# Turns by PE's transpose mode, a 64-row attention tile by pairs of heads, a decay term read from SBUF, and ranks averaged in the planner

## The chip, the core and the metric

One core of a Trainium2 chip. The metric is the device time of one execution in microseconds (us). Engines: PE (TensorE; PEld is its weight load), DVE (VectorE), ACT (ScalarE), POOL (GpSimd), SP (SyncE, whose queue issues the DMAs).

## What is computed

Attention with a decay, then two MLPs, for 4 x 576 tokens. Cut to what matters:

```
scores = q @ k.T / 8 + cum[:, None] - cum[None, :]    # 4 batches, 8 heads, 576 rows, 64 wide; cum = cumsum(log(clip(f)))
attn   = softmax(causal(scores)) @ v                  # float32 inputs
h = x @ w_in;  x = (h * tanh(softplus(h))) @ w_out    # 512 -> 2048 -> 512, weights float64
h = x @ w2_in; s = h * softmax(h)                     # 512 -> 1024 -> 512
out = (layernorm(s) * g_ln) @ w2_out
```

cum of the query row is the same for a whole row of the softmax, so only the key's part, -cum, is added.

## The kernel before, in words

Tokens stand in tiles of 128 rows. Each batch has five tiles of queries (NCH); in batch 0 the last one has 64 rows. `seq` lists attention steps (batch, tile, heads): four heads at a time in the first tile, two in the second, one in the others. Each step runs `step_s` (scores, L511), `step_r` (row maximum on DVE, exponentials on ACT, L535), `step_h` (the probabilities cut into two fp16 halves by ACT and POOL, then transposed by a DMA, L570) and `step_pv` (products with v, L607); `fin` (L640) divides by the row sums, cuts the result and transposes it by DMA into `xT`, the input of the first MLP.

Batch 0 is special. Its q and k are fp32 and are turned by `turn` (L394): PE multiplies a block by the fp32 identity (L399), ACT copies the result from PSUM (L403, L405). In its first two tiles the probabilities are turned in the same way. Scores are a group of products in `scores` (L479): q by k in fp32 (L500), then the decay (L501) as an fp16 product of 67 rows, of which 64 are zero and three are ones (`qb`) that meet the three fp16 parts of -cum in rows 64 to 66 of `ktr`, one row set a head; on the diagonal the mask is added by an identity product (L505). The decay is made on chip by a scan (L268), cut into three fp16 parts, written to DRAM (`dd`, L274) and read back into `ktr` by a DMA for each key chunk (L414).

In the last tile of a batch the 64-column end of the keys has its own scores for all eight heads first (into `sps[2]`), then each head has 512 columns.

PE's other work: gram products of the weights (L148), the low halves of early weights (`h_lo`, L192 and L193), the first MLP (`up`, L887; `down`, L931), the second MLP (L1686, and L1763, where the output has seven products). DVE converts the float64 weights (L125 to L129).

The program is written in one order and then reordered: `Order` (L1108) models every operation's cost (`weigh`, `duration`), makes orders by a list schedule forward (`plan`) with ranks that a backward pass gives (`back`), twelve rounds at each of two slowdowns, replays every order found with random delays, and pins the order with the least time on each engine (`pin`, L1568). How much attention is put between the MLP's steps is set by `att_slots` from `cost` (L984). Engines run their own queues in the pinned order and wait on semaphores.

Of the kernel before, what the change touches and what calls it, by code (L numbers as in the profile page):

```python
# [211 lines left out]
def emit(tc, q, k, v, f, w_in, w_out, w2_in, w2_out, g_ln, out):  # L212
# [14 lines left out]
        fill=MASKED, base=0, channel_multiplier=1,  # L227
    )
    ones = const.tile([P, P], F32, name="ones")
    nc.gpsimd.memset(ones, 1.0)  # L230
# [35 lines left out]
    nc.vector.memset(ft, 1.0)  # L266
    dt_ = rp0.tile([B * H, S], F32, name="dt_")
    nc.vector.tensor_tensor_scan(dt_, ft, lf, 0.0, op0=ALU.mult, op1=ALU.subtract)  # L268
# [17 lines left out]
    for i in range(2):  # L286
        nc.gpsimd.memset(qb[i][64:96], 1.0)
    for t in q32:
        nc.gpsimd.memset(t[64:, :, 0], 0.0)
        nc.gpsimd.memset(t[:64, :, 1], 0.0)  # L290
# [103 lines left out]
    def turn(dst, src, r0, r1_, nm, scale=1.0):  # L394

        t = psh.tile([P, 2, TB], F32, tag="h", name=f"h_{nm}").rearrange("p g (y s) -> p (g y) s", s=P)
        n = src.shape[-1] // P
        for y in range(n):
            nc.tensor.matmul(  # L399
                t[:, y, r0:r1_], src[r0:r1_, y * P:(y + 1) * P], ident32[r0:r1_, r0:r1_], start=True, stop=True)  # L400
        if type(dst) is list:
            for y, d in enumerate(dst):
                nc.scalar.activation(d[:, :, r0:r1_], t[64 * y:64 * y + 64, :, r0:r1_], AF.Copy, scale=scale)  # L403
            return
        nc.scalar.copy(dst[:, :n, r0:r1_], t[:, :n, r0:r1_])  # L405

    def split_k(b, c):
        r0, r1_, t0 = rows_of(b, c)
        n = r1_ - r0
        if b == 0:  # L410
            x = (b * NCH + c) % NKT
            turn(kt32[:, x, :4], raw["k", b, c], r0, r1_, f"k{c}")
            kt[b, c] = ktr[:, x]
            nc.sync.dma_start(  # L414
                ktr[64:67, x, H:, r0:r1_],
                dd[b * H:(b + 1) * H, :, t0:t0 + n].rearrange("h j s -> j h s"),
            )
            return
        t = kn[cnt["kn"] % KNB]
        cnt["kn"] += 1  # L420
        t3 = t[:, :H * P].rearrange("p (h d) -> p h d", h=H)
        rk = hd(raw["k", b, c][r0:r1_])
        s = sc["k", b][r0:r1_]
        split(nc, t3[r0:r1_, :, 64:], t3[r0:r1_, :, :64], rk, s, qmode(b, c, 0))
        kc = ktr[:, (b * NCH + c) % NKT]
        kt[b, c] = kc
        nc.sync.dma_start_transpose(out=kc[:, :H, r0:r1_], in_=t[r0:r1_, :H * P])
        nc.vector.tensor_copy(kc[:64, H:, r0:r1_], kc[64:, :H, r0:r1_])  # L428
        nc.sync.dma_start(
            kc[64:67, H:, r0:r1_],  # L430
            dd[b * H:(b + 1) * H, :, t0:t0 + n].rearrange("h j s -> j h s"),
        )
# [13 lines left out]
    def split_q(b, c):  # L446
        r0, r1_, t0 = rows_of(b, c)
        if b == 0:
            qa = q32[c % 2]
            turn([qa[:64, :, 0], qa[64:, :, 1]], raw["q", b, c], r0, r1_, f"q{c}", 0.125)  # L450
            qt[b, c] = qa, qb[0]
            return
        t = attd.tile([P, H, P], F16, tag="qn", name=f"qn_{b}_{c}", bufs=1)
        rq = hd(raw["q", b, c][r0:r1_])
        s = sc["q", b][r0:r1_]
        split(nc, t[r0:r1_, :, :64], t[r0:r1_, :, 64:], rq, s, qmode(b, c, 2))
        qa = qat[:, cnt["qb"] % 2].rearrange("p (h s) -> p h s", s=P)
        nc.sync.dma_start_transpose(out=qa[:, :, r0:r1_], in_=t[r0:r1_].rearrange("p h d -> p (h d)"))
        qb_ = qb[cnt["qb"] % 2]
        cnt["qb"] += 1  # L460
        nc.vector.tensor_copy(qb_[:64, :, r0:r1_], qa[:64, :, r0:r1_])
        qt[b, c] = (qa, qb_)
# [16 lines left out]
    def scores(o, b, i, h, cs):  # L479

        r0, r1_, _ = rows_of(b, i)
        qa, qb_ = qt[b, i]
        for c0, c1 in runs(b, cs):
            a0, a1, _ = rows_of(b, c0)
            w = 128 * (c0 - cs[0])
            s = (b * NCH + c0) % NKT
            n = c1 - c0
            d = o[:, w + a0 - o0(b, cs):w + 128 * (n - 1) + a1 - o0(b, cs)]
            k = ktr[:, s:s + n]
            k2 = k[:67, :, H + h]  # L490
            if b:
                q1, k1 = qa[:, h, r0:r1_], k[:, :, h]
            else:
                q1, k1 = qa[:, h // 2, h % 2, r0:r1_], kt32[:, s:s + n, h // 2]
            if n > 1:
                d = d.rearrange("p (c s) -> p c s", s=P)
            else:
                k1, k2 = k1[:, 0, a0:a1], k2[:, 0, a0:a1]
            diag = c1 == i + 1
            nc.tensor.matmul(d, q1, k1, start=True, stop=False)  # L500
            nc.tensor.matmul(d, qb_[:67, h, r0:r1_], k2, start=False, stop=not diag)  # L501
            if diag:
                a0, a1, _ = rows_of(b, i)
                w = 128 * (i - cs[0]) - o0(b, cs)
                nc.tensor.matmul(o[:, w + a0:w + a1], ident[:, r0:r1_], maskd[:, a0:a1], start=False, stop=True)  # L505

# [4 lines left out]
    def step_s(b, i, hs):  # L511
# [5 lines left out]
        if i < NCH - 1:  # L517
# [3 lines left out]
            for g, h in enumerate(hs):  # L521
                cs = range(i + 1)
                o = sp[:m, wd * g + o0(b, cs):wd * (g + 1)]
                scores(o, b, i, h, cs)
        else:
            if hs[0] == 0:
                assert banks() == 3
                for h in range(H):
                    scores(sps[2][:m, 64 * h:64 * (h + 1)], b, i, h, [0 if off else i])
            sp = sps[cnt["s"] % 2]  # L530
# [4 lines left out]
    def step_r(b, i, hs):  # L535
# [13 lines left out]
        if i < NCH - 1:  # L549
# [6 lines left out]
            return  # L556
        h = hs[0]
        ex = sps[2][:m].rearrange("p (h s) -> p h s", h=H)
        if h == 0:
            ne = attd.tile([P, H], F32, tag="ne", name=f"ne_{b}", bufs=1)  # L560
            nc.vector.tensor_reduce(ne[:m], ex, axis=AX.X, op=ALU.max, negate=True)
            pend["ne", b] = ne
# [7 lines left out]
    def step_h(b, i, hs):  # L570
        m, pt = pend.pop(("p", b, i, hs))
        n = len(hs) * (i + 1)
        if b == 0 and i < 2:
            pT = attd.tile([P, 4 * NCH, P], F16, tag="pT", name=f"pT_{b}_{i}_{hs[0]}", bufs=PTB)
# [4 lines left out]
        h0, o = hs[0], 0  # L579
        if n == i + 1 and h0 % 2:  # L580
            h0 -= 1
            o = n
            ph = pend.pop(("ph", b, i))
        else:
            ph = attd.tile([P, 4 * NCH, P], F16, tag="ph", name=f"ph_{b}_{i}_{h0}", bufs=PHB)
# [12 lines left out]
        nc.gpsimd.tensor_tensor(p4[:, :, 1], pv3, p4[:, :, 0], op=ALU.subtract)  # L598
        if n == i + 1 and o == 0:
            pend["ph", b, i] = ph  # L600
            return
# [5 lines left out]
    def step_pv(b, i, hs):  # L607
# [20 lines left out]
        for g, h in enumerate(hs):  # L628
            o = acc[:m, h * D:(h + 1) * D]
            for c in range(i + 1):  # L630
                a0, a1 = (0, P) if i else rows_of(b, c)[:2]
                vc = vt[b, c]
                vh = vc[a0:a1, 0, h * D:(h + 1) * D]
                vl = vc[a0:a1, 1, h * D:(h + 1) * D]
                k = 2 * (g * (i + 1) + c)
                nc.tensor.matmul(o, pT[a0:a1, k, :m], vh, start=(c == 0), stop=False)  # L636
                nc.tensor.matmul(o, pT[a0:a1, k, :m], vl, start=False, stop=False)  # L637
                nc.tensor.matmul(o, pT[a0:a1, k + 1, :m], vh, start=False, stop=(c == i))  # L638

    def fin(b, i):  # L640
# [4 lines left out]
        rr = attd.tile([P, H], F32, tag="rr", name=f"rr_{b}_{i}", bufs=2)  # L645
        st = 1 if i == NCH - 1 else 2
        nc.vector.tensor_reduce(
            rr[:m], rs[:m, 0:3:st].rearrange("p j h -> p h j"), axis=AX.X, op=ALU.add)
        nc.vector.reciprocal(rr[:m], rr[:m])
        x32 = attd.tile([P, DM], F32, tag="x32", name=f"x32_{b}_{i}", bufs=1)  # L650
# [85 lines left out]

    seq = []
    for b in range(B):
        for i, g in enumerate(GRP):
            seq += [(b, i, tuple(range(h, h + g))) for h in range(0, H, g)]  # L740
    pos = {"k": 0, "pv": 0}

# [234 lines left out]
    for j in range(NBLK):  # L977
        last = (j + 1) * TB - 1
        b, t = divmod(last, S)
        i = (t + OFF[b]) // P  # L980
        need.append(b * sum(H // g for g in GRP) + sum(H // g for g in GRP[:i + 1]))
    assert need[0] == n0

    def cost(n):  # L984
        b, i, hs = seq[n]
        return (128 * (i + 1) + 60) * len(hs)

# [95 lines left out]
LANDED = 600.0  # L1083
ROUNDS = 12
SEEDS = 8
# [22 lines left out]
class Order:  # L1108
# [141 lines left out]
    def weigh(self):  # L1250

        for o in self.ops:
            if o.eng == "PE":
                o.rows = [next(b for t, b, w in acc if not w).ap[0][1] > 64 for i, acc in o.ins]
                o.d = SWITCH * sum(a != b for a, b in zip(o.rows, o.rows[1:]))
                for i, acc in o.ins:
                    c = elems(next(b for t, b, w in acc if w)) / 2.4
                    if size_of(next(t for t, b, w in acc if not w).dtype) == 4:
                        c = max(4.0 * c, 224.0)
                    o.cols += c  # L1260
# [307 lines left out]
    def pin(self):  # L1568
        found = []
        for f in SLOW:  # L1570
            self.slower(f)
            rank = [o.k for o in self.ops]
            for _ in range(ROUNDS):
                found.append(self.plan(rank))
                rank = self.back()
        self.slower(1.0)
# [261 lines left out]
```

## Time and profile before

| | us |
|---|---|
| median of 3 runs | 769.73 |
| lowest and highest | 769.17, 769.89 |
| profiled execution | 770.08 |
| its span, first to last instruction | 766.9 |
| PE busy in it | 736.0 |

Busy times are unions of instruction spans; a matmul's end is modelled, so matmuls in a row overlap in their spans, and what one of them costs is read from start to start. An fp32 product stands as two records. Granted clock 1.00 is 2.4 GHz, 0.50 is 1.2 GHz.

### The profile page before, as it was taken

How to read it: one execution, taken by the hardware profiler on the slowest of the kernel's cores; microseconds unless marked ns; L12 is line 12 of the kernel's file. 1: busy time of each engine (PE TensorE's matmuls, PEld its weight loads, DVE VectorE, ACT ScalarE, POOL GpSimd, SP SyncE). 2: the span in 40 equal slices, each digit the busy share in tenths (PEclk: the TensorE clock that was granted, in tenths of full speed). 3: DMA queues.
4: the chain of work that ended last, by engine and by line, in shares of the span. 5: the costliest groups of instructions: out<-in, count | busy, mean ns of one | idle time of the engine just before them, and what ended most of it. 6: DMA issues, size and time to landing. Idle time of an engine off the chain costs nothing.

```text
span 766.9 us, 17022 instructions
## 1 busy us (share of the span) xinstructions
PE 736.0 (96%) x6346; PEld 509.6 (66%) x6346; DVE 582.0 (76%) x1201; ACT 605.7 (79%) x1315; POOL 424.3 (55%) x368
## 2 busy tenths in 40 slices
PE   4999999999998999999999999999999999999898
PEld 3776765566675677766778777675754565566577
DVE  6988987888798887688778637798945776766564
ACT  3686999988998989998998968997766656767550
POOL 6013356577766786775787933314213565877721
PEclk9999999999998999999999999999999999999999
DMA  9979777899769999989988446530022678778765
GB/s 272 288 224 250 221 130 129 149 167 173 181 148 187 168 174 204 177 152 174 175 163 161 89 84 174 185 127 12 20 51 56 117 143 149 155 146 165 136 146 137
DMA packets 317118, 118.06 MB, mean 154 GB/s; under 512 B 302380, under 2 KB 303148, under 8 KB 317036
## 3 DMA queue, kind: packets, MB, share of 16 engines
q1 hardware_dynamic: 317036, 116.99, 73.0%
q8 instruction: 49, 0.80, 0.4%
q14 instruction: 33, 0.27, 0.1%
HBM read 46.59 MB, written 9.55 MB: 73 GB/s over the span
## 4 chain that ended last, share of the span: by engine, by line
PE 58%; ACT 10%; DMA 10%; DVE 9%; POOL 7%; issue 6%; SPq 0%; ACTq 0%; POOLq 0%; DVEq 0%
PE x L931 15%; PE h L887 15%; PE o L1763 7%; PE h L1686 5%; PE sp L500 4%; PE sp L501 2%; DMA win<-za 2%; DMA x2d<-x2h 2%; POOL s L1724 2%; POOL gt L914 2%; PE h_lo L192 2%; POOL ph L598 2%; DMA wi_r<-in_moe_w_in_dram 1%; DMA pT<-ph 1%; PE pv L636 1%
## 5 line engine op out<-in xcount | busy, mean ns | idle before, releaser
L931 PE MATMUL x<-wout,gt 128*128 128x512 f16 x864 | 214.7, 382 | 5.1 <-POOL gt L914 2.9
L887 PE MATMUL h<-xT,win 128*128 128x256 f16 x1728 | 210.2, 273 | 1.3 <-ACT th L900 1.3
L887 PEld LDWEIGHTS <-win 128*128 128x128 f16 x1728 | 166.5, 98 | 39.2 <-issue 2.9
L598 POOL TENSOR_TENSOR ph<-p,ph 128x512 f16<-128x512 f32 (+4 forms) x114 | 149.2, 1314 | 60.8 <-ACT ph L597 46.1
L914 POOL TENSOR_TENSOR gt<-th,gt 128x512 f16<-128x512 f32 x72 | 96.6, 1343 | 109.6 <-ACT gt L913 109.5
L931 PEld LDWEIGHTS <-gt 128*128 128x128 f16 x864 | 79.7, 98 | 78.4 <-issue 6.2
L1686 PE MATMUL h<-w,x2T 128*128 128x512 f16 x432 | 95.7, 379 | 0.1
L908 DVE SCALAR_TENSOR_TENSOR th<-ta,th 128x512 f32<-128x512 f32 x72 | 55.7, 774 | 25.9 <-ACT ta L907 21.6
L1686 PEld LDWEIGHTS <-x2T 128*128 128x128 f16 x432 | 42.1, 98 | 49.0 <-issue 0.7
L553 ACT ACTIVATE p<-sp,nm 64x64 f32<-64x64 f32 (+7 forms) x128 | 62.2, 492 | 7.9 <-DVE nm L551 6.0
L551 DVE TENSOR_REDUCE nm<-sp 128x1 f32<-128x320 f32 (+7 forms) x88 | 49.1, 564 | 24.0 <-PE sp L505 15.5
L899 ACT ACTIVATE ta<-h,cols 128x512 f32<-128x512 f32 (+3 forms) x96 | 54.3, 580 | 15.8 <-PE h L887 15.8
L659 POOL TENSOR_TENSOR xh<-x,xh 128x512 f16<-128x512 f32 (+1 forms) x20 | 27.9, 1394 | 65.1 <-DVE xh L658 64.7
L501 PE MATMUL sp<-ktr,qb 67*128 67x64 f16 (+6 forms) x304 | 59.5, 241 | 1.7 <-DVE ktr L428 1.7
L500 PE MATMUL sp<-ktr,qat 128*128 128x64 f16 (+7 forms) x288 | 54.3, 260 | 2.0 <-ACT p L568 2.0
L913 ACT CAST gt<-th 128x512 f16<-128x512 f32 x72 | 44.7, 621 | 11.3 <-DVE th L908 6.7
L904 DVE TENSOR_SCALAR ta<-ta 128x512 f32<-128x512 f32 x72 | 47.1, 655 | 8.7 <-ACT ta L899 8.1
L906 ACT ACTIVATE ta<-ta,cols 128x512 f32<-128x512 f32 x72 | 52.0, 723 | 0.5
L905 ACT ACTIVATE ta<-ta 128x512 f32<-128x512 f32 x72 | 45.5, 633 | 8.2 <-DVE ta L904 8.2
L636 PE MATMUL pv<-vt,pT 128*128 128x64 f16 (+2 forms) x456 | 50.2, 196 | 0.3 <-DMA pT<-ph 0.2
L638 PE MATMUL pv<-vt,pT 128*128 128x64 f16 (+2 forms) x456 | 50.0, 195 | 0.0
L637 PE MATMUL pv<-vt,pT 128*128 128x64 f16 (+2 forms) x456 | 50.0, 195 | 0.0
(272 smaller groups left out, 1641.6 us busy)
## 6 DMA issues: line engine op xcount, KB each, us to landing
wi_r<-in_moe_w_in_dram SPq DMA_DIRECT2D x8, 1024.0 KB
wo_r<-in_moe_w_out_dram SPq DMA_DIRECT2D x8, 1024.0 KB
x2d<-x2h SPq DMA_DIRECT2D x18, 256.0 KB
out_dram<-ro SPq DMA_DIRECT2D x18, 256.0 KB
w2i_r<-in_moe_w_in_dram SPq DMA_DIRECT2D x4, 1024.0 KB
w2o_r<-in_moe_w_out_dram SPq DMA_DIRECT2D x4, 1024.0 KB
rawv<-in_v_dram SPq DMA_DIRECT2D x13, 256.0 KB
rawk<-in_k_dram SPq DMA_DIRECT2D x13, 256.0 KB
```

What stands on the lines that cost most here:

```text
L500: nc.tensor.matmul(d, q1, k1, start=True, stop=False)
L501: nc.tensor.matmul(d, qb_[:67, h, r0:r1_], k2, start=False, stop=not diag)
L553: nc.scalar.activation(pv[:m, g * (i + 1) * P + off:g * (i + 1) * P + end], s3[:, g, off:end], AF.Exp, bias=nm[:m, g:g + 1], accum_out=rs[ ...
L598: nc.gpsimd.tensor_tensor(p4[:, :, 1], pv3, p4[:, :, 0], op=ALU.subtract)
L636: nc.tensor.matmul(o, pT[a0:a1, k, :m], vh, start=(c == 0), stop=False)
L887: nc.tensor.matmul(ph, win[:, (fi // 4) * NC1 + c, col:col + P], x[:, lx * NC1 + c, :], start=(m == 0), stop=(m == 3 * NC1 - 1))
L899: nc.scalar.activation(ta[:, :, a:e], ph[:, :, a:e], AF.Exp, scale=usc(b, fi // 4))
L908: nc.vector.scalar_tensor_tensor(th, ta, 2.5, th, op0=ALU.subtract, op1=ALU.mult)
L914: nc.gpsimd.tensor_tensor(gt[:, 1], th, gt[:, 0], op=ALU.subtract)
L931: nc.tensor.matmul(o, gt[:, lg, n % 2, t * P:(t + 1) * P], wout[:, fi, lw * 512:(lw + 1) * 512], start=(first and m == 0), stop=(last and ...
L1686: nc.tensor.matmul(h[:, half * 512:(half + 1) * 512], x[:, lx * NC1 + c, :], self.w2[:, half * NC1 + c, lw * 512:(lw + 1) * 512], start=(n ...
L1763: nc.tensor.matmul(o, z[nm][:, (2 * at + lz) * q + c, :], self.wo[:, form, lw, c], start=(n == 0), stop=(n == 3 * q - 1))
```

## The change

- `turn` uses PE's transpose mode in place of a product with the identity.
- Batch 0's last tile: two heads are stacked, one in rows 0 to 63 and one in rows 64 to 127. The q turn puts the even head's 64 rows at columns 64 to 127 of its block, so that 128 neighbouring columns hold both heads. The decay then has six rows, three a head, and `pick`, a block of ones in `qb[0]`, gives each half its three; the DMA of the decay writes six rows for four pairs. `mask2` is the 64-wide mask twice. Maxima, exponentials, halves and transposes run once a pair; `fin` brings the pair's reciprocals back to 64 rows. `qb[0]` is set to ones again before batch 1 uses it.
- The first two tiles take their decay from the scan's fp32 tile in SBUF, padded with zeros to 128 rows, by a product with one column of the identity broadcast to 128; their key chunks are no longer taken together.
- The planner: a transpose counts 112 ns, the ranks are the mean of the last four backward passes, and there are twenty rounds.

The diff, without its context lines:

```diff
@@ -226,6 +226,9 @@
+    mask2 = const.tile([P, D], BF16, name="mask2")
+    for y in range(0, P, D):
+        nc.vector.tensor_copy(mask2[y:y + D], maskd[y:y + D, y:y + D])
@@ -264,7 +267,10 @@
-    dt_ = rp0.tile([B * H, S], F32, name="dt_")
+    dtp = rp0.tile([P, S], F32, name="dt_")
+    for y in range(B * H, P, B * H):
+        nc.gpsimd.memset(dtp[y:y + B * H, :2 * P], 0.0)
+    dt_ = dtp[:B * H]
@@ -285,6 +291,11 @@
+    pick = qb[0][:70, :2].rearrange("p h s -> p (h s)")
+    for i, (m, o) in enumerate(((-1, 2), (1, -3))):
+        x = qb[0][64:96, i]
+        nc.gpsimd.affine_select(
+            out=x, in_=x, pattern=[[0, P]], compare_op=ALU.is_ge, fill=0.0, base=o, channel_multiplier=m)
@@ -396,11 +407,11 @@
-            nc.tensor.matmul(
-                t[:, y, r0:r1_], src[r0:r1_, y * P:(y + 1) * P], ident32[r0:r1_, r0:r1_], start=True, stop=True)
+            nc.tensor.transpose(t[:, y, r0:r1_], src[r0:r1_, y * P:(y + 1) * P], ident32[r0:r1_, r0:r1_])
-                nc.scalar.activation(d[:, :, r0:r1_], t[64 * y:64 * y + 64, :, r0:r1_], AF.Copy, scale=scale)
+                o = 0 if y or r1_ == P else P - r1_
+                nc.scalar.activation(d[:, :, r0 + o:r1_ + o], t[64 * y:64 * y + 64, :, r0:r1_], AF.Copy, scale=scale)
@@ -412,8 +423,8 @@
-                ktr[64:67, x, H:, r0:r1_],
-                dd[b * H:(b + 1) * H, :, t0:t0 + n].rearrange("h j s -> j h s"),
+                ktr[64:70, x, H::2, r0:r1_],
+                dd[b * H:(b + 1) * H, :, t0:t0 + n].rearrange("(x y) j s -> (y j) x s", y=2),
@@ -448,7 +459,7 @@
-            qt[b, c] = qa, qb[0]
+            qt[b, c] = qa, pick
@@ -457,6 +468,8 @@
+        if (b, c) == (1, 1):
+            nc.gpsimd.memset(qb_[64:96, :2], 1.0)
@@ -480,29 +493,37 @@
-        for c0, c1 in runs(b, cs):
+        for c0, c1 in runs(b, cs) if b or i > 1 else [(c, c + 1) for c in cs]:
-            k2 = k[:67, :, H + h]
+            one, low = ident[:, r0:r1_], maskd
-                q1, k1 = qa[:, h, r0:r1_], k[:, :, h]
+                q1, k1, q2, k2 = qa[:, h, r0:r1_], k[:, :, h], qb_[:67, h, r0:r1_], k[:67, :, H + h]
-                q1, k1 = qa[:, h // 2, h % 2, r0:r1_], kt32[:, s:s + n, h // 2]
+                x, y = divmod(h, 2)
+                q1, q2 = qa[:, x, y, r0:r1_], qb_[:, y * P + r0:y * P + r1_]
+                if i == NCH - 1:
+                    q1, q2 = qa[:, x].rearrange("p y s -> p (y s)")[:, D:D + P], qb_[:, D:D + P]
+                    one, low = ident, mask2
+                k1, k2 = kt32[:, s:s + n, x], k[:70, :, H + 2 * x]
+                if i < 2:
+                    q2 = ident32[:, h:h + 1].to_broadcast([P, P])
+                    k2 = dtp[:, c0 * P:c1 * P].rearrange("p (c s) -> p c s", s=P)
-            nc.tensor.matmul(d, qb_[:67, h, r0:r1_], k2, start=False, stop=not diag)
+            nc.tensor.matmul(d, q2, k2, start=False, stop=not diag)
-                nc.tensor.matmul(o[:, w + a0:w + a1], ident[:, r0:r1_], maskd[:, a0:a1], start=False, stop=True)
+                nc.tensor.matmul(o[:, w + a0:w + a1], one, low[:, a0:a1], start=False, stop=True)
@@ -523,10 +544,13 @@
+            if b == 0:
+                m = P
-                for h in range(H):
-                    scores(sps[2][:m, 64 * h:64 * (h + 1)], b, i, h, [0 if off else i])
+                for h in range(0, H, len(hs)):
+                    x = h // len(hs)
+                    scores(sps[2][:m, 64 * x:64 * (x + 1)], b, i, h, [0 if off else i])
@@ -554,11 +578,11 @@
-        h = hs[0]
+        h, nh = hs[0] // len(hs), H // len(hs)
-            nc.vector.tensor_reduce(ne[:m], ex, axis=AX.X, op=ALU.max, negate=True)
+            nc.vector.tensor_reduce(ne[:m, :nh], ex[:, :nh], axis=AX.X, op=ALU.max, negate=True)
@@ -570,6 +594,8 @@
+        if b == 0 and i == NCH - 1:
+            n = i + 1
@@ -577,7 +603,7 @@
-        if n == i + 1 and h0 % 2:
+        if len(hs) == 1 and h0 % 2:
@@ -596,7 +622,7 @@
-        if n == i + 1 and o == 0:
+        if len(hs) == 1 and o == 0:
@@ -627,15 +653,17 @@
+            both = b == 0 and i == NCH - 1
+            x = slice(D * g, D * g + m) if both else slice(m)
-                k = 2 * (g * (i + 1) + c)
-                nc.tensor.matmul(o, pT[a0:a1, k, :m], vh, start=(c == 0), stop=False)
-                nc.tensor.matmul(o, pT[a0:a1, k, :m], vl, start=False, stop=False)
-                nc.tensor.matmul(o, pT[a0:a1, k + 1, :m], vh, start=False, stop=(c == i))
+                k = 2 * (0 if both else g * (i + 1)) + 2 * c
+                nc.tensor.matmul(o, pT[a0:a1, k, x], vh, start=(c == 0), stop=False)
+                nc.tensor.matmul(o, pT[a0:a1, k, x], vl, start=False, stop=False)
+                nc.tensor.matmul(o, pT[a0:a1, k + 1, x], vh, start=False, stop=(c == i))
@@ -644,9 +672,15 @@
+        n, w = (P, H // 2) if b == 0 and i == NCH - 1 else (m, H)
-            rr[:m], rs[:m, 0:3:st].rearrange("p j h -> p h j"), axis=AX.X, op=ALU.add)
-        nc.vector.reciprocal(rr[:m], rr[:m])
+            rr[:n, :w], rs[:n, 0:3:st, :w].rearrange("p j h -> p h j"), axis=AX.X, op=ALU.add)
+        nc.vector.reciprocal(rr[:n, :w], rr[:n, :w])
+        if w < H:
+            r2 = attd.tile([P, H], F32, tag="rr", name=f"rr2_{b}_{i}", bufs=2)
+            for y in range(2):
+                nc.vector.tensor_copy(r2[:m, y::2], rr[D * y:D * y + m, :w])
+            rr = r2
@@ -735,9 +769,12 @@
+    upto = {}
+            g = 2 if (b, i) == (0, NCH - 1) else g
+            upto[b, i] = len(seq)
@@ -978,12 +1015,12 @@
-        need.append(b * sum(H // g for g in GRP) + sum(H // g for g in GRP[:i + 1]))
+        need.append(upto[b, i])
-        return (128 * (i + 1) + 60) * len(hs)
+        return (128 * (i + 1) + 60) * (1 if i == NCH - 1 else len(hs))
@@ -1081,7 +1118,7 @@
-ROUNDS = 12
+ROUNDS = 20
@@ -1256,7 +1293,7 @@
-                        c = max(4.0 * c, 224.0)
+                        c = 112.0 if i.is_transpose else max(4.0 * c, 224.0)
@@ -1569,10 +1606,11 @@
-            rank = [o.k for o in self.ops]
+            rank, last = [o.k for o in self.ops], []
-                rank = self.back()
+                last = last[-3:] + [self.back()]
+                rank = [sum(x) / len(x) for x in zip(*last)]
```

## Rows read from the trace of the kernel before

**Rows 1.** The page's first part: busy us, share of the span, instructions.

```profile
PE 736.0 (96%) x6346; PEld 509.6 (66%) x6346; DVE 582.0 (76%) x1201; ACT 605.7 (79%) x1315; POOL 424.3 (55%) x368
```

**Rows 2.** Busy time by stretch: length, then PE, PEld, DVE, ACT, POOL, clock, DMA.

```profile
0.00:24.00 24.00, 13.23 (x70) 11.86 (x71) 17.34 (x40) 7.56 (x14) 12.09 (x25) 1.00 1.00 278
31.00:80.00 49.00, 48.95 (x323) 35.49 (x323) 43.48 (x93) 38.51 (x83) 9.61 (x6) 1.00 0.85 248
80.00:160.00 80.00, 77.92 (x787) 49.61 (x786) 67.88 (x137) 76.59 (x189) 48.10 (x38) 1.00 0.78 151
220.00:262.00 42.00, 36.92 (x401) 26.02 (x400) 35.99 (x77) 38.46 (x107) 27.26 (x26) 0.92 0.91 166
262.00:720.00 458.00, 453.96 (x3807) 306.91 (x3806) 336.22 (x701) 368.57 (x753) 265.73 (x222) 1.00 0.68 134
720.00:740.00 20.00, 17.00 (x119) 12.21 (x118) 11.09 (x29) 11.72 (x19) 12.28 (x10) 0.91 0.70 150
```

**Rows 3.** What PE waited for: us in total, times, longest.

```profile
PE h_k L399 <- DMA wout<-in_k_dram: 7.6, 1, 7.6
PE o L1763 <- ACT acc L1777: 3.0, 1, 3.0
PE x L931 <- POOL gt L914: 2.9, 3, 1.3
PE sp L500 <- ACT p L568: 2.0, 1, 2.0
PE sp L148 <- DVE win L129: 2.0, 2, 1.8
PE x L931 <- DVE x2h L960: 1.6, 1, 1.6
```

**Rows 4.** The turns (L399) by stretch: PE busy with records, PEld, clock, DMA.

```profile
0.00:24.00 24.00, 7.89 (x32) 7.11 (x32) 1.00 1.00 278
24.00:100.00 76.00, 13.01 (x96) 11.75 (x96) 1.00 0.82 235
```

**Rows 5.** Chain of waits: start, us, what (x records); first and last tile.

```profile
40.92 1.84 PE h_p L399 x16
42.76 0.43 PE sp L500 x2
43.19 0.11 PE sp L501
43.30 0.06 PE sp L505
...
110.69 0.14 PE sp L500 x2
110.90 0.14 PE sp L500 x2
...
114.00 1.00 PE sp L500 x2
115.00 0.22 PE sp L501
```

**Rows 6.** Single instructions of the start: start, us, engine, line, form.

```profile
10.38 1.34 DVE L268 TENSOR_TENSOR_SCAN dt__103<-ft,lf 32x576 f32<-32x576 f32 x1
13.56 1.20 ACT L403 ACTIVATE knt<-h_q 64x512 f32<-64x512 f32 x2 [3.33 <-PE h_q L399]
22.26 0.77 PE L500 MATMUL sp<-ktr,knt 128*128 128x128 f32 x2
23.76 0.44 PE L500 MATMUL sp<-ktr,knt 128*128 128x128 f32 x2
24.04 0.22 PE L501 MATMUL sp<-ktr,qb 67*128 67x128 f16 x1
```

**Rows 7.** PE in two stretches: busy, granted clock, DMA.

```profile
235.40:238.70 3.30, 3.30 (x31) 0.50 1.02 217
245.70:248.90 3.20, 3.20 (x40) 0.50 1.11 118
```

## The prediction

> **What bounds the kernel now.** I read the page's first part, then the engines by stretch, then what PE waited for, then the chain of waits and single instructions of the first 30 us. The reader should see in [rows 1] that PE is busy 736.0 of 766.9 us while no other engine passes 79%, and in [rows 2] where the rest lies: 10.8 us in the first 24 us (24 - 13.23), 0.05 in 31 to 80, 2.1 in 80 to 160, 5.1 in 220 to 262, 4.0 in 262 to 720 and 3.0 in 720 to 740. PE's longest waits [rows 3] say the same: the first load of k, then 3.0, 2.9, 2.0 and 1.6 us at four places late in the run, 9.5 us together. So PE's own work sets the time from about 31 us on, and an edit counts by what it takes from or adds to that work. In the first 100 us this is a narrow lead: DVE is busy 43.48 of the 49 us from 31 to 80, and ACT 76.59 of the 80 us from 80 to 160 [rows 2].
>
> The clock column of [rows 2] reads 1.00 in the first stretch, but the same pair of fp32 records takes 0.77 us at 22.26 and 0.44 us at 23.76 [rows 6]: TensorE ran at 1.2 GHz until then and at 2.4 GHz after it. Before the rise PE had worked on turns, gram products and scores with little rest. Two later stretches read 0.50 [rows 7]; the first follows one of the waits of [rows 3], the 2.0 us on ACT.
>
> **Part 1, the 64-row tile by pairs.** Batch 0's last tile makes scores for each of eight heads with 64 rows. One head costs PE 0.21 us for the 64 columns (110.69 to 110.90) and 1.22 us for the 512 columns (1.00 + 0.22) [rows 5]. Four pairs on 128 rows issue the same columns four times instead of eight: 4 x 1.43 = 5.7 us less; with the 0.86 us that such an fp32 pair takes elsewhere (0.43 for 256 columns, [rows 5]) in place of 1.00 it is 5.2. The products with v stay, 15 for each head. DVE, ACT and POOL lose four of their eight rounds too, which frees the ACT that is nearly full in that stretch; I count that at nothing, since PE idles only 2.1 us there [rows 2]. Four transposing DMAs remain, each half as large. The two small copies that bring the reciprocals back to 64 rows are DVE work of tenths of a us, hidden by DVE's own 12.1 free us of 80.
>
> **Part 2, the transpose mode.** The turns issue 128 records, 32 before 24 us and 96 after it [rows 4]; a product of fp32 is two records, so 48 products lie where PE is the bound. Sixteen records in a row take 1.84 us [rows 5], 0.115 us a record and 0.23 a product. No row shows the mode. It could cost what the product costs now (nothing gained), or as little as a product of 128 by 128 in one pass, the 0.06 us of the mask [rows 5] (0.17 saved each, 8.2 us). I take one record, half of today's price, because the data are still fp32 and the diff's own constant of the planner (112 ns) is the same size: 48 x 0.115 = 5.5 us less. The Trainium skill ("TensorE: Matmul & The Clock Gate", Terms) calls the mode four times faster for FP32; by that a product would be an estimated 0.058 us, the term 8.3 and the sum 2.8 us lower; no run here shows it yet. The 16 products before 24 us lie beside waits for loads, and count for nothing here.
>
> **Part 3, the first decay on chip.** For the first two tiles the fp16 product with three decay rows becomes an fp32 product with 128 rows. In the first tile a head's fp32 product runs from 23.76 to 24.04, 0.28 us [rows 6], where an fp16 product of that width takes the mask's 0.06 [rows 5]; 0.23 (part 2) is the other price of such a product. Added: 8 x (0.17 to 0.22) = 1.4 to 1.8. In the second tile the two key chunks are no longer taken together: four fp32 products of 0.23 to 0.28 replace 0.43 + 0.11 [rows 5]: 8 x (0.38 to 0.58) = 3.0 to 4.6. Together 4.4 to 6.4 more; I take 5.2, near the lower price since most of these follow one another.
>
> In return the scores no longer wait for the decay's way out to DRAM and back. The decay is on chip at 11.72 (10.38 + 1.34) and the first q is copied at 14.76 (13.56 + 1.20), while the first score starts at 22.26 [rows 6]. PE stands still about 2.6 us in between, for gram inputs and the v statistics (2.0 of it in [rows 3]). Filling that with scores at 1.2 GHz brings half of it, some 1.5 us; nothing if DVE, which makes both the gram inputs and the maxima, stays the later one, 3 if the clock rises earlier as well. I take 1.5. The DMAs of the decay keep their number and their piece count (24 a chunk); they only land before the third tile needs them. The new memsets and selects go to POOL, busy 12.09 of the first 24 us [rows 2]; if that cover were gone they would cost a few us at most, as the 25 instructions there now take 12.09 together. The later memset for batch 1 waits on POOL for the last scores of batch 0, with subtractions of that tile queued behind it; PE has other work in 80 to 160.
>
> **Part 4, averaged ranks and twenty rounds.** This changes the order of everything and no work. What it can win is the late waits and the low clock behind them: 9.5 us [rows 3] and half of the 3.3 and 3.2 us at half clock [rows 7], 3.2 us: 12.7 in all, of which an order that mends two thirds would win 8. What it can lose is one more such place: 720 to 740 lost 3.0 us of PE time, and about 1.7 in clock, 4.7. From -8 to +5; I take 0, since nothing in the rows says which way a new order moves these waits.
>
> **The sum.** -5.7 - 5.5 + 5.2 - 1.5 = -7.5 us. The profiled execution took 770.08 us, 3.2 outside its span and 0.35 above the median of 769.73; 770.08 - 7.5 = 762.6, so 762.2 as a median. A measurement here can tell about 0.2%, 1.5 us, from no change.
>
> **Rivals.** First, the stalls go as well. For it: a smaller ACT load through batch 0's last tile lets attention run ahead, and one of the late waits (2.0 us) is on ACT's exponentials. Against: those waits are in batch 1 and in the last stage, which the edit does not touch. It gives 762.2 - 8 = 754.2; chance 0.18.
>
> Second, the gain is eaten. If the mode costs what the product costs (0 for 5.5), the decay is at its dear end (6.4) and nothing is won at the start, the sum is -5.7 + 6.4 = +0.7, 770.4. DVE at 43.48 of 49 us speaks for it too: PE's lighter early work may just wait for the weight conversions. Against: PE's 0.05 us of idle in that stretch shows nothing late. Chance 0.10.
>
> Third, slower: the turns in the new mode leave the clock low. Today the clock stays up through all turns after 24 us; those are ordinary products. If PE's activity as the clock sees it does not include a transpose, each of the 12 bursts of four after 24 us could bring a stretch as in [rows 7], 1.65 us each (half of 3.3). The Trainium skill (same page, Part 4: PE-mode transpose) says that the full clock does not engage for the transpose mode; by that rule this rival would hold, and so far the trace has no row on it. It decides from six such stretches on: 6 x 1.65 = 9.9, and 762.2 + 9.9 = 772.1. Against: a burst lasts under 1.84 us between scores and pv products, and the low stretch of [rows 7] came after a full stop of 2.0 us. Chance 0.07.
>
> **How the numbers follow.** The forecast has 0.65, with a range of its own from 757 to 767. The range given goes from 753, the first rival with a cheaper mode, to 769.5, the dear decay with half of the mode's gain; it leaves out the third rival, part of the second, and stalls beyond half of the sum of late waits. Faster by over 0.2%: 0.65 + 0.18 = 0.83; within: 0.10; slower: 0.07.
>
> **What would show it.** Turn records: half as many, or as long as half, beginning with the k turn. Scores at 64 columns: four groups of records. The first score near 15 to 17 us, the clock up no later than 24 us, and no idle in 31 to 80. Late waits near 9.5 us in total. I am wrong if PE's idle before 160 us grows by several us (DVE or ACT late), if a stretch at half clock stands behind the turns, or if the late waits double.

## The result and the profile after

The changed kernel takes 757.52 us (median of 5, 757.16 to 757.70) against 769.73 us (median of 5 beside it): a ratio of 0.9839, 95% interval 0.9825 to 0.9854, or 12.2 us less where 7.5 were forecast. The profiled execution took 757.16 us, its span is 755.4.

The page's first part of the changed kernel, which answers to [rows 1]:

```profile
PE 723.7 (96%) x6302; PEld 502.3 (66%) x6302; DVE 583.6 (77%) x1197; ACT 600.9 (80%) x1295; POOL 415.8 (55%) x370
```

PE is still the bound, with 12.3 us less busy time. Over the whole span it rests 31.7 us (755.4 - 723.7) where it rested 30.9: the gain is shorter work, the clock's share in it included, and not less rest. The stretches of [rows 2] in the changed kernel, with the same columns, and one that goes on to 755 us:

```profile
0.00:24.00 24.00, 11.68 (x77) 9.76 (x78) 18.23 (x28) 7.68 (x17) 12.92 (x28) 1.00 0.98 280
31.00:80.00 49.00, 48.68 (x341) 33.88 (x338) 44.30 (x96) 41.29 (x86) 12.89 (x10) 1.00 0.89 255
80.00:160.00 80.00, 75.99 (x765) 51.13 (x763) 68.73 (x144) 74.02 (x174) 45.83 (x38) 0.98 0.81 160
220.00:262.00 42.00, 38.15 (x430) 27.54 (x428) 36.01 (x69) 38.99 (x104) 28.47 (x26) 0.96 0.95 170
262.00:720.00 458.00, 453.78 (x3756) 305.84 (x3754) 342.30 (x707) 368.14 (x748) 263.52 (x222) 1.00 0.66 133
720.00:740.00 20.00, 19.10 (x175) 16.82 (x173) 13.20 (x35) 10.00 (x17) 8.42 (x7) 1.00 0.88 170
720.00:755.00 35.00, 30.89 (x279) 26.90 (x276) 19.50 (x48) 10.92 (x18) 8.42 (x7) 1.00 0.76 151
```

From 31 to 80 us PE has hardly any rest (0.3 us), as before. From 80 to 160 it rests 4.0 us where it rested 2.1, and the clock falls once there. From 720 to 740 us the clock stays at 1.00 where [rows 2] has 0.91, and PE works 19.10 us where it worked 17.00. What PE waited for, answering to [rows 3]:

```profile
PE h_k L410 <- DVE win L125: 7.2, 1, 7.2
PE sp L522 <- DVE qb L474: 2.9, 1, 2.9
PE x L968 <- POOL gt L951: 2.6, 3, 1.3
PE sp L148 <- DVE win L129: 2.5, 2, 1.4
PE pv L664 <- DMA pT<-ph: 2.2, 4, 1.2
...
PE sp L521 <- ACT p L592: 1.8, 2, 0.9
PE h L1724 <- DVE s2c L1741: 1.3, 1, 1.3
PE o L1801 <- DVE acc L1808: 0.9, 2, 0.6
```

The wait of 3.0 us in the second MLP's output is gone; waits for a copy of q (2.9) and for transposing DMAs (2.2) have come. Where the gain stands along the way is read from the last start of a kind of product: the first MLP's `up` ends at 581.5 us in the kernel before,

```profile
L887 PE MATMUL h<-xT,win x1728: 269/273/283, 70.9 to 581.5; 128*128 128x256 f16 x192
```

and at 573.2 in the changed one, which starts it 2.7 us sooner:

```profile
L924 PE MATMUL h<-xT,win x1728: 269/273/421, 68.2 to 573.2; 128*128 128x256 f16 x192
```

So 8.3 us are won by then, and 11.5 (766.9 - 755.4) at the end. The last 3.2 us lie behind it, in the rest of `down` and the second MLP, where the edit changes no work. From the end of `up` to that of the span, before and after, PE has the same 1188 instructions:

```profile
581.50:766.80 185.30, 177.50 (x1188) 116.42 (x1186) 122.38 (x321) 109.26 (x189) 107.26 (x85) 0.99 0.71 140
573.20:755.40 182.20, 176.19 (x1188) 115.69 (x1185) 119.93 (x319) 109.23 (x190) 106.99 (x85) 1.00 0.74 141
```

It is busy 1.3 us less there, without the fall of the clock, and rests 6.0 us in place of 7.8.

The parts, in the changed kernel's trace. Turns by stretch, in the columns of [rows 4]:

```profile
0.00:24.00 24.00, 4.38 (x16) 2.86 (x16) 1.00 0.98 280
24.00:100.00 76.00, 6.92 (x48) 5.14 (x48) 1.00 0.87 239
```

Half as many records. Single instructions of PE (start, us, line, form): a turn of k, two heads of the first tile, a turn of its probabilities and one head's group of the second tile, then pairs of the 64-row tile:

```profile
16.58 1.09 PE L410 MATMUL h_k<-ident,wout 128*128 128x128 f32 x4 [2.08 <-DMA wout<-in_k_dram]
...
18.56 0.63 PE L521 MATMUL sp<-ktr,knt 128*128 128x128 f32 x2
19.06 0.77 PE L522 MATMUL sp<-dt__106,ident 128*128 128x128 f32 x2
...
20.40 0.44 PE L521 MATMUL sp<-ktr,knt 128*128 128x128 f32 x2
20.68 0.39 PE L522 MATMUL sp<-dt__106,ident 128*128 128x128 f32 x2
20.90 0.22 PE L526 MATMUL sp<-maskd,ident 128*128 128x128 bf16 x1
20.96 0.44 PE L521 MATMUL sp<-ktr,knt 128*128 128x128 f32 x2
...
24.65 0.61 PE L410 MATMUL h_p<-ident,p 128*128 128x128 f32 x4
25.10 0.28 PE L367 MATMUL sum<-sctv,ones 128*128 128x1 f32 x2
...
27.94 0.39 PE L521 MATMUL sp<-ktr,qat 128*128 128x128 f32 x2
28.16 0.39 PE L522 MATMUL sp<-dt__106,ident 128*128 128x128 f32 x2
28.39 0.39 PE L521 MATMUL sp<-ktr,qat 128*128 128x128 f32 x2
28.61 0.39 PE L522 MATMUL sp<-dt__106,ident 128*128 128x128 f32 x2
28.83 0.22 PE L526 MATMUL sp<-maskd,ident 128*128 128x128 bf16 x1
28.89 0.44 PE L521 MATMUL sp<-ktr,qat 128*128 128x128 f32 x2
...
109.30 0.41 PE L521 MATMUL sp<-ktr,knt 128*128 128x64 f32 x2
109.61 0.41 PE L521 MATMUL sp<-ktr,knt 128*128 128x64 f32 x2
...
117.98 1.10 PE L521 MATMUL sp<-ktr,knt 128*128 128x512 f32 x2
118.93 0.38 PE L522 MATMUL sp<-ktr,qb 70*128 70x512 f16 x1
119.15 1.02 PE L521 MATMUL sp<-ktr,knt 128*128 128x512 f32 x2
```

The same groups of the first and the second tile in the kernel before:

```profile
24.16 0.44 PE L500 MATMUL sp<-ktr,knt 128*128 128x128 f32 x2
...
24.55 0.44 PE L500 MATMUL sp<-ktr,knt 128*128 128x128 f32 x2
...
29.18 0.60 PE L500 MATMUL sp<-ktr,qat 128*128 128x256 f32 x2
...
29.79 0.65 PE L500 MATMUL sp<-ktr,qat 128*128 128x256 f32 x2
```

Four turned blocks take 0.45 us (24.65 to 25.10), 0.11 each. A head of the first tile takes 0.56 us (20.40 to 20.96) where it took 0.39 (24.16 to 24.55). A head of the second tile takes 0.95 us (27.94 to 28.89) where it took 0.61 (29.18 to 29.79). A pair takes 0.31 us for 64 columns and 1.17 for 512 (117.98 to 119.15). The first score and its decay lie 0.50 us apart (18.56 to 19.06) and the third 0.28 (20.40 to 20.68), so TensorE went from 1.2 to 2.4 GHz in between, though the clock column reads 1.00 for the whole first stretch, as in [rows 2].

### The profile page after: what moved, and what is told of

The parts are those of the page before. It is cut to its first block, busy times and chain, and to the rows that moved or that the text cites. A ratio compares the mean times of both kernels' runs of the same rounds, so it can differ in the third digit from the quotient of the medians.

```text
span 755.4 us, 16941 instructions
## 1 busy us (share of the span) xinstructions
PE 723.7 (96%) x6302; PEld 502.3 (66%) x6302; DVE 583.6 (77%) x1197; ACT 600.9 (80%) x1295; POOL 415.8 (55%) x370
## 5 line engine op out<-in xcount | busy, mean ns | idle before, releaser
L924 PE MATMUL h<-xT,win 128*128 128x256 f16 x1728 | 213.8, 274 | 0.1
L624 POOL TENSOR_TENSOR ph<-p,ph 128x512 f16<-128x512 f32 (+3 forms) x110 | 138.2, 1264 | 61.0 <-ACT ph L623 50.9
L951 POOL TENSOR_TENSOR gt<-th,gt 128x512 f16<-128x512 f32 x72 | 93.3, 1297 | 114.4 <-ACT gt L950 110.9
L945 DVE SCALAR_TENSOR_TENSOR th<-ta,th 128x512 f32<-128x512 f32 x72 | 59.9, 833 | 15.9 <-ACT ta L944 15.6
L521 PE MATMUL sp<-ktr,qat 128*128 128x64 f16 (+7 forms) x304 | 56.1, 256 | 2.5 <-ACT p L592 1.8
L522 PE MATMUL sp<-ktr,qb 67*128 67x64 f16 (+7 forms) x280 | 52.9, 239 | 3.6 <-DVE qb L474 2.9
L941 DVE TENSOR_SCALAR ta<-ta 128x512 f32<-128x512 f32 x72 | 44.4, 618 | 9.6 <-ACT ta L936 9.4
L664 PE MATMUL pv<-vt,pT 128*128 128x64 f16 (+2 forms) x456 | 49.2, 194 | 2.4 <-DMA pT<-ph 2.2
L619 POOL TENSOR_SCALAR ph<-p 128x512 f16<-128x512 f32 (+3 forms) x45 | 33.5, 745 | 32.0 <-ACT p L577 18.2
L664 PEld LDWEIGHTS <-pT 128*128 128x128 f16 (+2 forms) x456 | 41.8, 100 | 12.2 <-DMA pT<-ph 4.4
```

The costliest lines, as they stand in the source:

```text
L522: nc.tensor.matmul(d, q2, k2, start=False, stop=not diag)
L664: nc.tensor.matmul(o, pT[a0:a1, k, x], vh, start=(c == 0), stop=False)
L924: nc.tensor.matmul(ph, win[:, (fi // 4) * NC1 + c, col:col + P], x[:, lx * NC1 + c, :], start=(m == 0), stop=(m == 3 * NC1 - 1))
L945: nc.vector.scalar_tensor_tensor(th, ta, 2.5, th, op0=ALU.subtract, op1=ALU.mult)
L951: nc.gpsimd.tensor_tensor(gt[:, 1], th, gt[:, 0], op=ALU.subtract)
```

## The experiments

Since every edit makes the planner draw another order, runs were of two kinds: versions with an order of their own, and versions held to the changed kernel's order. Each ratio is that to the kernel before run beside it, with its 95% interval; versions that did not run beside each other are compared by their ratios. The theories at the start: **A**, the edits of the work are worth about the forecast's 7.5 us and the order the rest; **B**, the work is worth all of it; **C**, the averaged ranks are.

**The planner's part alone, on the kernel before** (`pin` with the mean of the last four ranks, `ROUNDS = 20`).

> The kernel before with the planner's part alone (mean of the last four ranks, twenty rounds), PE's work as before. Theory A (the three edits of the work are worth the 7.5 us of the prediction, the other 4.7 us are the order's, which took away the stall of 720 to 740 us): about 765.0. Theory B (the edits of the work are worth all 12.2 us, the order nothing): 769.7, within 1.5. Theory C (most of the gain is the averaging's): 762 or less.

Measured: 771.06 us, ratio 1.0014 (0.9997 to 1.0032). The stall after 720 us went in this version too (its longest wait in that stage is 1.5 us), yet others came, such as 2.3 us on DVE before a product with v. C falls, and A's 765 was wrong as well; B's 769.7 fits, since on the old work the averaging wins nothing.

**The planner's part undone in the changed kernel.**

```diff
-                last = last[-3:] + [self.back()]
-                rank = [sum(x) / len(x) for x in zip(*last)]
+                rank = self.back()
```

> The changed kernel with the planner's old ranks and twelve rounds; the work is the changed one. Theory A: 757.5 + 4.7 = 762.2. Theory B: 757.5, within 1.5. Theory C: 765 or more.

Measured: 759.76 us, ratio 0.985 (0.983 to 0.987). By the ratio that is 758.2 where the kernel before takes 769.73, so B fits here too, and the interval overlaps the changed kernel's.

**Other orders of the same work** (`SLOW = (1.02, 1.05)`).

> The changed kernel's work in another order: the planner's two slowdowns are 1.02 and 1.05 in place of 1.03 and 1.06. If an order is a draw that is worth some us: a time that differs from 757.5 by 2 to 6 us, with the stalls behind 100 us in other places. If the averaged search finds much the same time whatever its constants: within 1.5 of 757.5.

> The kernel before in another order, by the same two slowdowns of 1.02 and 1.05. If an order is a draw: 2 to 6 us from 769.7. If not: within 1.5 of it. With the run of the averaged ranks (771.1) it gives the spread of three orders of the same work.

Measured: the changed work 764.26 us, ratio 0.9904 (0.9867 to 0.994); the old work 772.51, ratio 1.0015 (0.9991 to 1.004). So three orders of the changed work gave ratios from 0.984 to 0.990, and three of the old one from 1.000 to 1.0015. By these ratios an order is worth up to 5 us on the changed work, more than B allows, and no order of either comes near the other's range: the gain is the work's by its greater part.

**Turns by products, in an order of their own.**

```diff
-            nc.tensor.transpose(t[:, y, r0:r1_], src[...], ident32[r0:r1_, r0:r1_])
+            nc.tensor.matmul(t[:, y, r0:r1_], src[...], ident32[r0:r1_, r0:r1_], start=True, stop=True)
```

> The changed kernel with turns by products with the identity again. The trace after shows a turn of four at 0.46 us in place of 0.92. If PE's work sets the time: 757.5 + 48 x 0.115 = 763.0. If DVE and ACT are what is late in the first 100 us and PE's shorter turns only make it wait: 757.5 to 759.

Measured: 757.05 us, ratio 0.9816 (0.9794 to 0.9838): no loss at all. Either the mode is worth nothing, or this order was a better draw.

**The same products in the changed kernel's own order.** The planner is told 112 ns for them, and then PE's instructions stand in the same order as in the changed kernel.

```diff
-                        c = 112.0 if i.is_transpose else max(4.0 * c, 224.0)
+                        c = 112.0 if next(t.name for t, b, w in acc if w).startswith(("h_k", "h_q", "h_p")) else max(4.0 * c, 224.0)
```

> The changed kernel with turns by products, but with the planner told the transpose's 112 ns for them, so that every engine's order is the changed kernel's own. If the mode is worth its work and the run with products in an order of its own (757.05) only drew a better order: 757.5 + 48 x 0.115 = 763.0, at least 761. If that run is right and the mode is worth nothing: 757.5, within 1.5. By the rule that a transpose does not count for the clock, the rise, at 20.0 us in the changed kernel, comes some us earlier here; if it counts, no earlier.

Measured: 759.47 us, ratio 0.9846 (0.9812 to 0.988). To compare on one chip, this version ran once more beside the changed kernel.

> The changed kernel itself, beside the next two on the same chip: 757.5, the clock up at about 20 us.

> Turns by products in the changed kernel's own order, a second time, now beside the changed kernel. If the mode's 6.6 us of PE work reach the end: 763. If part of it is paid back by a clock that rises sooner, as the first look (rise at 15.2 us) says: 759 to 760, the rise before 17 us again. If the first look's rise was chance: the rise at 19 to 21 us and 761 or more.

Measured: the changed kernel 756.79 us (753.72 to 757.65), the products 758.21 (757.78 to 758.39); ratios 0.9833 (0.9808 to 0.9858) and 0.9858 (0.984 to 0.9876). With one order, the lag of the products can be followed. Last starts of gram products and of `up`, in the profiled executions of the changed kernel first,

```profile
L148 PE MATMUL sp<-wout x64: 217/218/233, 23.7 to 93.3; 128*128 128x128 bf16 x64
```

of its second run,

```profile
L148 PE MATMUL sp<-wout x64: 218/218/233, 24.1 to 93.7; 128*128 128x128 bf16 x64
L924 PE MATMUL h<-xT,win x1728: 269/273/421, 68.5 to 569.5; 128*128 128x256 f16 x192
```

and of the products beside it:

```profile
L148 PE MATMUL sp<-wout x64: 218/218/232, 23.8 to 99.2; 128*128 128x128 bf16 x64
L924 PE MATMUL h<-xT,win x1728: 269/273/421, 71.4 to 573.7; 128*128 128x256 f16 x192
```

At the last gram product the products are 5.9 and 5.5 us late: the forecast's term has reached that point in full. At the end of `up` they are late by 4.2 us against one execution of the changed kernel and by 0.5 against the other (573.7 - 573.2). Part of what takes the lead back is seen in the waits. From 330 to 440 us the first execution of the changed kernel has

```profile
PE pv L664 <- DMA pT<-ph: 1.4, 2, 1.2
```

while neither its second execution nor the products have that wait; at 132.8 to 135.8 us its granted clock is 0.50,

```profile
132.80:135.80 3.00, 3.00 (x25) 0.50 0.47 89
```

and in the other two it is 1.00 there. Such waits and falls differ between two executions of one program, too. By the medians on one chip 1.4 us of 5.5 are left, and the intervals of the two ratios overlap; by these pairs of traces 1.2 to 4.6 are left (spans 756.6 against 755.4 and 752.0).

**The first 16 turns alone by products**, in the changed kernel's order (the turns named k0, k1, q0, q1).

> The changed kernel's own order, with products for the 16 turns of the first two chunks of k and q alone and transposes for the other 48. If transposes do not count for the clock: the rise at 14 to 17 us in place of 20, and 755.5 to 757, the lower work kept. If the rise does not hang on the mode: the rise at 20 us and 757.5 to 758, the 16 products lying beside waits for loads.

Measured: 756.22 us, ratio 0.9829 (0.9808 to 0.985), no difference from the 756.79 beside it. The eight records of the second k turn take 1.13 us at 16.24, so TensorE was at 2.4 GHz by then; a score at 19.68 takes 0.74 us again, as at the low level, so it fell in between. The turn of the same place is seen at both levels with all turns by products: in the first run, on one chip,

```profile
16.12 1.13 PE L410 MATMUL h_k<-ident,wout 128*128 128x128 f32 x8 [1.16 <-DMA wout<-in_k_dram]
```

and in the second, on another,

```profile
16.14 2.05 PE L410 MATMUL h_k<-ident,wout 128*128 128x128 f32 x8 [1.64 <-DMA wout<-in_k_dram]
```

In both profiled executions of the changed kernel the first scores, at 18.56 and 18.16, still ran at the low level. That leans towards the third rival's premise, that the clock's activity does not include a transpose. The other traces of the changed work lean the same way: with products a score takes 0.44 us at 15.74 (the version with an order of its own), with transposes still 0.74 at 20.91 (decay from DRAM), 21.98 (old ranks) and 22.43 (other order). But the old work, all products, has 0.74 at 23.04 as well. With such a spread it isn't settled, and no time hangs on it here.

**The 64-row tile head by head.**

```diff
-            g = 2 if (b, i) == (0, NCH - 1) else g
...
-            both = b == 0 and i == NCH - 1
+            both = False
```

(with the other edits of that part undone likewise).

> The changed kernel with batch 0's last tile head by head on 64 rows. PE's work rises by 4 x (0.21 + 1.07 to 1.22) = 5.1 to 5.7 us. If work counts and orders draw about 3 us either way: 757.5 + 5.4 = 762.9, from 760 to 766. If the tile lies beside other work: 757.5, within 3.

Measured: 768.77 us, ratio 0.9992 (0.9962 to 1.0021). By the ratios that is some 12 us more than the changed kernel, twice the work that came back. Its profiled span is 11.0 us longer (766.4): PE is busy 726.4 us, only 2.7 more, and rests 40.0 (766.4 - 726.4) where it rested 31.7. Its waits show where:

```profile
PE sp L148 <- DVE win L129: 10.1, 2, 9.7
PE pv L657 <- DMA pT<-ph: 5.8, 6, 1.5
PE sp L148 <- DVE wout L129: 5.0, 2, 4.7
```

The 9.7 us are the wait before PE's first instruction, which is 7.2 in the changed kernel. A poor draw at the start and more waits for transposing DMAs come with the 5.7 us of work. If the work counts in full, some 6 us are the draw, more than the 5 us between the three orders above. How much of the 12 us the pairs themselves bring is not parted here, and no run has the pairs alone.

**The decay of the first two tiles from DRAM**, key chunks together.

```diff
-                if i < 2:
-                    q2 = ident32[:, h:h + 1].to_broadcast([P, P])
-                    k2 = dtp[:, c0 * P:c1 * P].rearrange("p (c s) -> p c s", s=P)
...
-        for c0, c1 in runs(b, cs) if b or i > 1 else [(c, c + 1) for c in cs]:
+        for c0, c1 in runs(b, cs):
```

> The changed kernel with the decay of the first two tiles read back from DRAM as an fp16 product again, key chunks together. PE's work falls by 8 x 0.16 + 8 x 0.33 = 3.9 us (a head of the first tile takes 0.555 us in the changed kernel and 0.395 before; of the second about 0.98 and 0.65). If the early start is worth 1.5 us as predicted: 757.5 - 3.9 + 1.5 = 755.1. If the early start is what the part pays for (clock up 3.8 us sooner, scores 3.7 us sooner): 758 to 761.

Measured: 755.15 us, ratio 0.9803 (0.9774 to 0.9832), as the predicted sum has it. This version drew an order of its own too, so the match is partly luck. `up` starts at 68.0 us in it, against 68.2, though the decay's extra work is gone: by then the early decay has paid back about its price. With the first 16 turns by products in addition it drew another order:

> Pairs and transposes with the decay from DRAM (755.15 alone) and products for the first 16 turns, in an order of its own. If the clock rises sooner as well: 753 to 755. If the order drawn decides: from 752 to 759, with the work the least of all versions (PE 3.9 us below the changed kernel, but for the 16 products).

Measured: 758.88 us, ratio 0.9869 (0.9847 to 0.989). The two lie on either side of the changed kernel; an early decay shows no gain, and 755.15 is the lowest median of all versions, though its interval overlaps the changed kernel's. It was not run beside it.

## Why the prediction was right, and where it was off

The measured 757.5 lies at the edge of the forecast's own range (757 to 767). Two of the four terms held, two were off by several us, and some 3 us given back on the way hide part of that, so the nearness of the time owes something to luck.

**What bounds it** held: PE is busy 96% of the span in both, and 31 to 80 us has hardly any rest in either (0.05 and 0.32 us), so the fear that DVE would be late there (second rival) did not come true; DVE rose to 44.30 of 49 us and PE still worked 48.68.

**Part 1** held: 8 x (0.21 + 1.22) = 11.4 us became 4 x (0.31 + 1.12 on average) = 5.7 (two of the four 512-wide pairs have 1.08, two 1.16), 5.7 less, as forecast.

**Part 2** held in its price: 0.11 us a turned block, where 0.115 was taken, and 5.5 to 5.9 us of lag without it at 93 us. That such a term reaches the end unchanged was too simple: on one chip 1.4 us of it did, by medians, hardly more than the noise. The Trainium skill ("TensorE: Matmul & The Clock Gate", Terms) has FP32 transposes four times faster; here the records are half as many and take the time that a record took, so the measurement says twice.

**Part 3** cost 1.0 us less than forecast: a head of the first tile costs 0.165 us more (0.56 against 0.39), a head of the second 0.365 (1.00 on average, from 0.95 to 1.03, against 0.63, from 0.60 to 0.66), 4.2 together, where 5.2 was taken and 4.4 was the lower bound. The step that failed is the price of 0.23 to 0.28: in a row of such products one takes 0.22, start to start, and 0.28 only follows after a short product.

The early start was mis-sized as well. The first score starts at 18.56, not at 15 to 17, because the order puts the second gram product and the turns of the second chunk before it, and those turns waited 2.08 us for k. `up` starts 2.7 us sooner though three things together add 1.4 by then: the turns (24 of p and 8 of the third chunk, 32 x 0.115 = 3.7 less), the decay (4.2 more), and 16 more gram products that the changed order puts ahead (88 against 72, 0.06 each, 0.9 more). So the early start is worth some 4.1 us by this estimate, above the 1.5 taken and above its bound of 3. In the first 31 us PE rests 12.0 us before and 12.3 after, so that stretch alone doesn't show rest being filled; with products in the same order it rests 10.0. So about 2 us of rest are filled, as the prediction had it, and the shorter early turns, which it counted at nothing, only widen the rest again. The other 2 us fit the clock, up 3.7 us sooner (20.0 against 23.7): half of that is 1.8, an estimate.

**Part 4** is a mis-sized term: 0 was taken. The stall of 720 to 740 us, priced in the prediction at 4.7 us with its clock, is gone, but behind `up` only 3.2 us are won, since other waits came (3.2 of the 4.1 us of rest from 720 to 755 lie behind 740). Against it stand longer waits from 80 to 160 us. Its bounds (-8 to +5) held, and the orders that were run show why no better value was to be had: the averaging gained nothing on the old work and, by the ratios, 0.8 us on the new, within the spread of orders.

The sum by measured terms: -5.7 - 5.5 + 4.2 - 4.1 - 3.2 = -14.3, of which 11.5 are seen in the span; some 3 us are given back on the way, 1.9 of them in PE's rest from 80 to 160 us (4.0 against 2.1, [rows 2]). These are the terms of one order against one other; what one edit alone brings at the end, with the order held, was measured for the turns only.

**The first rival** (754.2) had part of its mechanism right, a late stall that goes, but its time lies below the measured one. **The third** did not come: no fall of the clock stands behind a turn. The two at 132.8 and 235.2 us follow waits for POOL and DVE, and the turns from 24 to 100 us run at 2.4 GHz (0.11 us a record against about 0.21 before the rise). In the other order of the changed work the clock reads 0.50 from 94.8 us, right after a turn at 94.67, but a wait of 1.63 us for POOL ends at 93.02; the old work in its other order has the same from 96.5, behind waits of 0.82 and 0.89 us and no turn. By the Trainium skill's rule (same page, Part 4: PE-mode transpose) the full clock would not engage; here it stays up through all 48 turns after 24 us.

Some of the prediction's working does not come out as it stands. With 0.86 us for an fp32 pair, part 1 would save 8 x 1.43 - 4 x 1.29 = 6.3 us, not 5.2. The rest between 11.72 and 22.26 us is 2.4 us (1.77 and 0.64), not 2.6. The 2.9 us of [rows 3] are three waits of at most 1.3, not one place. The ends of the range don't follow from the terms named for them: 754.2 with the cheaper mode is 751.5, not 753, and 762.2 with the dear decay and half of the mode's gain is 766.2, not 769.5. None of these decides the result.

## What to carry to other kernels

Where one engine sets the end, price an edit by the start-to-start distance of its instructions and expect the sum to arrive at the next place where that engine waits for another, not necessarily at the end: of 5.5 to 5.9 us at 93 us, 1.4 were left at the end by medians. A kernel whose order is searched for draws a new order with every edit, worth up to 5 us here: measure several orders, or hold the order by telling the planner the same costs, before an edit is called good or useless. In this case the version with products looked as fast as the transposes until both had the same order, and even then it was only 1.4 us slower, with overlapping intervals.

## What was not expected of the hardware

One program at one place ran eight records in 1.13 us in one execution and in 2.05 in another, on another chip: the clock's first rise moves by some us from run to run. And the first execution of the changed kernel lost 3.4 us to the second in its span (755.4 against 752.0), the larger part at one fall of the clock and at one wait of 1.2 us for a DMA that the second did not have.
